# Loads of x and w1 dealt over two DMA rings, and a new order of block 0, in a dense layer with Mish

## The chip, the cores and the metric

The kernel runs on one core of a Trainium2 chip. The metric is the time that the device takes for one execution, in microseconds (us). The profile's span runs from the first to the last instruction of the core and is a little shorter than that time.

## The reference

x is 2048 x 512, w1 is 512 x 1792, b1 has 1792 elements, w2 is 1792 x 512; everything is bf16.

```python
h = jnp.einsum("bsd,df->bsf", x, w1) + b1
sp = jnp.log1p(jnp.exp(-jnp.abs(h))) + jnp.where(h > 0, h, jnp.zeros_like(h))
act = h * jnp.tanh(sp)                      # Mish
return jnp.einsum("bsf,fd->bsd", act, w2)
```

## The kernel before, in words

The 2048 rows of x are worked in four blocks of 512 rows (s = 0 to 3, each of four x tiles of 128 rows). For each block, mm1 makes h transposed: for each of the 14 f tiles (128 columns of w1) four matmuls over k (512 = 4 x 128) add up into one bank of PSUM, with w1 as the weights and x transposed (xT) as the moving operand. ScalarE's Mish with b1 as bias (`mish`, L152) writes a_sb, in the layout that mm2 needs as weights. mm2 (L191) then adds up 14 matmuls for each tile of 128 output rows, VectorE copies the result out of PSUM (L197), and SP writes it out (L200).

The order is written out by hand. Each engine has a `Stream`: `mark` counts up the engine's semaphore, `wait` puts a wait in front of the engine's next instruction. `free[bank]` holds what must have read a bank before TensorE may start a new sum in it. The profile names the tiles w1_sb and w2_sb both w_sb, b1_nat b_nat, b1_pad b_pad, b1_sb b_sb.

Loads. All use the helper at L84. ScalarE issues two parts of w1, f tiles 0-3 (F0 = 4) with k 0-1 and with k 2-3 (256 KB each), and then loads its table (L122). SP issues x tiles 0-1 in one load (x_nat, 256 KB; each partition takes two neighbouring rows, so the block's rows come interleaved and `rows` at L180 undoes that in the output), then a DMA transpose of x tiles 2-3 straight into xT (x23), f tiles 4-7 in two parts, b1, the rest of w1, w2, and the DMA transposes of blocks 1 to 3.

Block 0. TensorE runs seven dummy matmuls on a constant (WARM, L128) while it waits for x_nat. `transpose_x` (L135) then transposes x tiles 0-1 with eight TensorE transposes (L142); VectorE and ScalarE copy two banks each into xT (L145). `first` makes f tiles 0-3 in banks 4-7, first for x tiles 0-1 over all k, then for tiles 2-3. VectorE meanwhile copies b1 into b1_pad (L230). `half` makes f tiles 4-6 with k 0-1 in banks 0-2. Then TensorE transposes b1 into bank 3 (L234), and VectorE copies it to b1_sb (L236), which every Mish needs. Then `half` with k 2-3, and from f tile 7 on whole f tiles by `mm1`.

Of the kernel before, what the change touches and what calls it, by code (L numbers as in the profile page):

```python
# [4 lines left out]

P = 128
WARM = (512,) * 5 + (256, 256)
BLOCKS = (512, 512, 512, 512)


# [21 lines left out]
def bass_standalone__dense_activation_mish__prompt_kernel(  # L32
# [8 lines left out]
    ACT = mybir.ActivationFunctionType  # L41
    ALU = mybir.AluOpType
    BF, F32 = dt.bfloat16, dt.float32
# [3 lines left out]
    KT, FT = D // P, F // P  # L47
    assert (S, D, F) == (2048, 512, 1792) and sum(BLOCKS) == S
    x2, out2 = x[0], out[0]
# [3 lines left out]
    F0 = 4  # L53
    N0 = BLOCKS[0] // P

    with ExitStack() as es:
        def sb(name, shape, t):
            return es.enter_context(nc.sbuf_tensor(name, shape, t))

        x_nat = sb("x_nat", [P, 2, D], BF)  # L60
        xT = sb("xT", [P, KT, S], BF)
        w1_sb = sb("w1_sb", [P, KT, F], BF)
        w2_sb = sb("w2_sb", [P, FT, D], BF)
        b1_nat = sb("b1_nat", [FT, P], BF)
# [3 lines left out]
        ident = sb("ident", [P, P], BF)  # L68
        a_sb = sb("a_sb", [P, FT, S], BF)
        o_sb = sb("o_sb", [P, S // P, D], BF)  # L70
        ps = es.enter_context(nc.psum_tensor("ps", [P, 8, 512], F32))

        def sem(name):
            return es.enter_context(nc.semaphore(name))

        sp = Stream(nc.sync, None)
        pe = Stream(nc.tensor, sem("c_pe"))
        dve = Stream(nc.vector, sem("c_dve"))
        act = Stream(nc.scalar, sem("c_act"))
        pool = Stream(nc.gpsimd, sem("c_pool"))  # L80

        def load(q, dst, src, name, transpose=False):
            s = sem(name)
            (q.eng.dma_start_transpose if transpose else q.eng.dma_start)(dst, src).then_inc(s, 16)  # L84
            return (s, 16)

        def load_w1(q, ks, a, b):
            return load(q, w1_sb[:, ks, a * P:b * P], w1v[:, ks, a * P:b * P], "s_w1_%d_%d" % (ks.start, a))

        t_w1, t_w2 = {}, {}

        def load_part(q, k0, k1, a, b):
            t = load_w1(q, slice(k0, k1), a, b)
            for f in range(a, b):
                for k in range(k0, k1):
                    t_w1[k, f] = t

        for k0, k1 in ((0, 2), (2, 4)):  # L100
            load_part(act, k0, k1, 0, F0)
        t_xn = load(sp, x_nat[:, :, :], x2[0:2 * P, :].rearrange("(p j) d -> p j d", p=P), "s_xn")
        t_x23 = load(sp, xT[:, :, 2 * P:4 * P], x2[2 * P:4 * P, :], "s_x23", True)
        for k0, k1 in ((0, 2), (2, 4)):
            load_part(sp, k0, k1, F0, 8)
        t_b1 = load(sp, b1_nat[:, :], b1.rearrange("(j p) -> j p", p=P), "s_b1")
        load_part(sp, 0, KT, 8, FT)
        t = load(sp, w2_sb[:, :, :], w2v, "s_w2")
        for f in range(FT):
# [2 lines left out]
        for s in range(1, len(BLOCKS)):  # L112
            lo, hi = starts[s], starts[s + 1]
# [6 lines left out]
        t_id = pool.mark(pool.eng.affine_select(ident[:, :], ones[:, :], pattern=[[1, P]], compare_op=ALU.is_equal,  # L120
                                                fill=0.0, base=0, channel_multiplier=-1))
# [5 lines left out]
        def dummy(n):  # L127
            nc.tensor.matmul(ps[:, 7, 0:n], c_w, c_m[:, 0:n], start=True, stop=True)  # L128


        free = [[] for _ in range(8)]
        t_cp = {(j, k): t_x23 for j in (2, 3) for k in range(KT)}
        t_mish, t_acc = {}, {}

        def transpose_x():  # L135

            pe.wait(t_xn, t_id)
            for k in range(KT):
                eng = (dve, act)[k % 2]
                psb = ps[:, k, 0:P].bitcast(BF)  # L140
                for j in range(2):
                    mm = nc.tensor.transpose(psb[:, j * P:(j + 1) * P], x_nat[:, j, k * P:(k + 1) * P], ident[:, :])  # L142
                eng.wait(pe.mark(mm))
                dst = xT[:, k, 0:2 * P]
                t = eng.mark(nc.vector.tensor_copy(dst, psb) if eng is dve else act.eng.activation(dst, psb, ACT.Copy))  # L145
                t_cp[0, k] = t_cp[1, k] = t
                free[k] = [t]

        def mish(s, f, bank, t_mm):
            n = BLOCKS[s]  # L150
            act.wait(t_b1c, t_mm)
            t = act.mark(act.eng.activation(a_sb[:, f, starts[s]:starts[s + 1]], ps[:, bank, 0:n], ACT.Mish,  # L152
                                            bias=b1_sb[:, f:f + 1]))
            t_mish[s, f] = t
            free[bank] = [t]

        def mm1_step(s, f, k, bank, js=None):

            n = BLOCKS[s]
            lo, hi = (0, n) if js is None else (js[0] * P, (js[-1] + 1) * P)  # L160
            first = k == 0 and lo == 0
            if first:
                pe.wait(*free[bank])
            pe.wait(t_w1[k, f])
            if s:
                pe.wait(t_xT[s])
            else:
                pe.wait(*[t_cp[j, k] for j in (js or range(N0))])
            return nc.tensor.matmul(ps[:, bank, lo:hi], w1_sb[:, k, f * P:(f + 1) * P],  # L169
                                    xT[:, k, starts[s] + lo:starts[s] + hi], start=first, stop=(k == KT - 1 and hi == n))  # L170

        def mm1(s, f, bank):
            for k in range(KT):
                mm = mm1_step(s, f, k, bank)
            mish(s, f, bank, pe.mark(mm))

        s_out = sem("s_out")
        n_out = 0

        def rows(i):  # L180

            if i < 2:
                return out2[0:2 * P, :].rearrange("(p j) d -> p j d", p=P)[:, i, :]
            return out2[i * P:(i + 1) * P, :]

        def mm2_step(i, f, lo, hi, bank):
            s = max(b for b in range(len(BLOCKS)) if starts[b] <= i * P)
            if f == 0:
                pe.wait(*free[bank])
            pe.wait(t_w2[f], t_mish[s, f])  # L190
            return nc.tensor.matmul(ps[:, bank, 0:hi - lo], a_sb[:, f, i * P:(i + 1) * P], w2_sb[:, f, lo:hi],  # L191
                                    start=(f == 0), stop=(f == FT - 1))

        def put(i, lo, hi, bank, t_mm):
            nonlocal n_out
            dve.wait(t_mm)
            t = dve.mark(nc.vector.tensor_copy(o_sb[:, i, lo:hi], ps[:, bank, 0:hi - lo]))  # L197
            free[bank] = [t]
            sp.wait(t)
            sp.eng.dma_start(rows(i)[:, lo:hi], o_sb[:, i, lo:hi]).then_inc(s_out, 16)  # L200
            n_out += 1

        def mm2(i, lo, hi, bank):
            for f in range(FT):
                mm = mm2_step(i, f, lo, hi, bank)
            put(i, lo, hi, bank, pe.mark(mm))


        def first(js, ks):
            for k in ks:  # L210
                for f in range(F0):
                    mm = mm1_step(0, f, k, 4 + f, js)
                    if k == KT - 1 and js[-1] == N0 - 1:
                        t_acc[f] = pe.mark(mm)

        def half(fs, ks):
            for f in fs:
                for k in ks:
                    mm = mm1_step(0, f, k, f - F0)
                if ks[-1] == KT - 1:  # L220
                    t_acc[f] = pe.mark(mm)

        for n in WARM:
            dummy(n)
        transpose_x()
        first((0, 1), range(KT))
        first((2, 3), range(KT))

        dve.wait(t_b1, t_bz)
        t_b1p = dve.mark(nc.vector.tensor_copy(b1_pad[0:FT, :], b1_nat[:, :]))  # L230
        half(range(F0, F0 + 3), (0, 1))
        pe.wait(t_b1p, *free[3])
        psb1 = ps[:, 3, 0:P // 2].bitcast(BF)
        t_b1t = pe.mark(nc.tensor.transpose(psb1, b1_pad[:, :], ident[:, :]))  # L234
        dve.wait(t_b1t)
        t_b1c = dve.mark(nc.vector.tensor_copy(b1_sb[:, :], psb1[:, 0:FT]))  # L236
        free[3] = [t_b1c]
        for f in range(F0):
            mish(0, f, 4 + f, t_acc[f])
        half(range(F0, F0 + 3), (2, 3))  # L240
        for f in range(F0, F0 + 3):
            mish(0, f, f - F0, t_acc[f])
        for f in range(F0 + 3, FT):
            mm1(0, f, (4 + f) % 8)

        for i in range(N0):
# [39 lines left out]
```

## Time and profile before

| what | value |
|---|---|
| median of 3 runs | 105.65 us (104.71 to 105.7) |
| the profiled execution | 105.38 us |
| its span | 104.1 us |
| TensorE matmuls busy | 100.8 us, 97% |
| ScalarE busy | 39.1 us, 38% |
| VectorE busy | 12.3 us, 12% |
| moved by DMA | 7.94 MB |

How to read it: PE is TensorE, PEld its weight loads, ACT ScalarE, DVE VectorE; SPq and ACTq are the instructions by which SP and ScalarE issue DMAs. A row of the timeline gives start, duration, engine, line, operation, the tile written and the tiles read, the shape, how often, and in brackets how long the engine was idle before it and what ended that. The chain of work is followed back from the last instruction, each step to what released it. A row of the windows gives the length of the stretch, the busy time of each engine with its number of instructions, the granted clock, the DMA share and GB/s. A row of a DMA queue gives packets, MB and share of the 16 engines' time in the window.

### The profile page before, as it was taken

The page shows a single profiled execution, that of the slowest core. Times are in us where ns is not written, and L with a number is a line of the kernel's source. Part 1 is how long each engine was busy: PE and PEld are TensorE (multiplying, and loading weights), DVE is VectorE, ACT ScalarE, POOL GpSimd, SP SyncE. Part 2 cuts the span into 40 slices and gives each one's busy share as a digit, 9 for nine tenths or more (in the row PEclk, how much of TensorE's full clock was granted, in tenths as well). Part 3 has the DMA queues.
Part 4 walks back from the last instruction along what each step waited for, and adds up shares of the span by engine and source line. Part 5 has one row for each costly group of instructions (what it writes and reads, how often), then busy time and mean ns, then how long its engine had stood idle before and what let it go on. Part 6 is the DMA issues. An engine that isn't in the chain of part 4 may idle for free.

```text
span 104.1 us, 1118 instructions
## 1 busy us (share of the span) xinstructions
PE 100.8 (97%) x485; PEld 48.2 (46%) x494; DVE 12.3 (12%) x22; ACT 39.1 (38%) x59; POOL 0.7 (1%) x6
## 2 busy tenths in 40 slices
PE   6999999999999999999999999999999999999992
PEld 2586444444444444444444444444444444444462
DVE  0200000022220000022220000022112000011223
ACT  3400999200027777200007777500005777700000
POOL 2000000000000000000000000000000000000000
PEclk9999999999999999999999999999999999999999
DMA  2999999991101000010111000001111000001111
GB/s 42 331 337 362 347 320 131 211 193 50 43 7 50 0 0 0 6 50 2 49 50 50 0 0 3 0 6 50 50 50 50 0 0 0 0 0 50 57 50 50
DMA packets 13345, 7.94 MB, mean 76 GB/s; under 512 B 7836, under 2 KB 13212, under 8 KB 13340
## 3 DMA queue, kind: packets, MB, share of 16 engines
q1 hardware_dynamic: 12796, 7.35, 27.0%
q10 hardware_dynamic: 544, 0.52, 1.4%
q8 instruction: 4, 0.07, 0.3%
q14 instruction: 1, 0.01, 0.0%
HBM read 3.94 MB, written 2.10 MB: 58 GB/s over the span
## 4 chain that ended last, share of the span: by engine, by line
PE 94%; DMA 3%; issue 1%; DVE 0%
PE ps L169 47%; PE ps L191 46%; DMA x_nat<-in_x_dram 3%; PE ps L142 1%; DVE o_sb L197 0%; PE ps L234 0%
## 5 line engine op out<-in xcount | busy, mean ns | idle before, releaser
L152 ACT ACTIVATE a_sb<-ps,b_sb 128x512 bf16<-128x512 f32 x56 | 37.1, 697 | 48.6 <-PE ps L169 43.3
L169 PE MATMUL ps<-xT,w_sb 128*128 128x512 bf16 (+1 forms) x235 | 49.3, 368 | 0.2
L191 PE MATMUL ps<-w_sb,a_sb 128*128 128x512 bf16 (+2 forms) x234 | 48.8, 366 | 0.3
L169 PEld LDWEIGHTS ps<-xT,w_sb 128*128 128x128 bf16 x240 | 23.7, 99 | 24.9
L191 PEld LDWEIGHTS ps<-w_sb,a_sb 128*128 128x128 bf16 x238 | 22.8, 98 | 25.9
L197 DVE CAST o_sb<-ps 128x512 bf16<-128x512 f32 (+2 forms) x17 | 11.2, 660 | 80.9 <-PE ps L191 80.9
L128 PE MATMUL ps<-const-bfloat16-1.0 128*128 128x512 bf16 (+1 forms) x7 | 2.7, 564 | 0.8 <-PEq L271 0.8
L122 ACT ACT_TABLE_LOAD x1 | 1.3, 1283 | 1.8 <-issue 1.8
L128 PEld LDWEIGHTS ps<-const-bfloat16-1.0 128*128 128x128 bf16 x7 | 0.9, 134 | 2.2 <-issue 2.2
L145 ACT ACTIVATE xT<-ps 128x256 bf16<-128x256 bf16 x2 | 0.8, 384 | 1.4 <-PE ps L142 1.3
L142 PE MATMUL ps<-ident,x_nat 128*128 128x128 bf16 x8 | 1.0, 311 | 0.2 <-DMA x_nat<-in_x_dram 0.2
L142 PEld LDWEIGHTS ps<-ident,x_nat 128*128 128x128 bf16 x8 | 0.8, 140 | 0.7 <-DMA x_nat<-in_x_dram 0.7
L145 DVE COPY xT<-ps 128x256 bf16<-128x256 bf16 x2 | 0.6, 292 | 3.3 <-PE ps L142 3.2
L230 DVE COPY b_pad<-b_nat 14x128 bf16<-14x128 bf16 x1 | 0.2, 183 | 3.1 <-DMA b_nat<-in_b_dram 3.1
L236 DVE CAST b_sb<-ps 128x14 f32<-128x14 bf16 x1 | 0.2, 173 | 2.2 <-PE ps L234 2.2
L120 POOL TENSOR_SCALAR_AFFINE_SELECT ident<-ones 128x128 bf16<-128x128 bf16 x1 | 0.3, 295 | 0.1
L234 PE MATMUL ps<-ident,b_pad 128*128 128x128 bf16 x1 | 0.2, 219 | 0.0
L117 DVE MEMSET b_pad<- 128x64 uint32 x1 | 0.1, 112 | 0.9 <-PEq L271 0.9
L118 POOL MEMSET ones<- 128x128 bf16 x1 | 0.2, 205 | 0.3 <-POOLq L271 0.3
L234 PEld LDWEIGHTS ps<-ident,b_pad 128*128 128x128 bf16 x1 | 0.1, 98 | 0.1
L271 POOL MEMSET const-bfloat16-1.0<- 128x1 bf16 x1 | 0.1, 102 | 0.0
L271 POOL MEMSET const-uint8-127<- 128x1 uint8 x1 | 0.1, 102 | 0.0
(2 smaller groups left out, 0.2 us busy)
## 6 DMA issues: line engine op xcount, KB each, us to landing
out_dram<-o_sb SPq DMA_DIRECT2D x15, 128.0 KB, 1.7
w_sb<-in_w_dram SPq DMA_DIRECT2D x1, 1792.0 KB, 10.4
w_sb<-in_w_dram SPq DMA_DIRECT2D x1, 768.0 KB, 5.6
w_sb<-in_w_dram ACTq DMA_DIRECT2D x2, 256.0 KB, 3.8
w_sb<-in_w_dram SPq DMA_DIRECT2D x2, 256.0 KB, 4.4
x_nat<-in_x_dram SPq DMA_DIRECT2D x1, 256.0 KB, 2.9
out_dram<-o_sb SPq DMA_DIRECT2D x1, 96.0 KB, 1.6
xT<-in_x_dram SPq DMA_TRANSPOSE x4, 5.5
```

The source lines that it names most:

```text
L118: t_ones = pool.mark(pool.eng.memset(ones[:, :], 1.0))
L120: t_id = pool.mark(pool.eng.affine_select(ident[:, :], ones[:, :], pattern=[[1, P]], compare_op=ALU.is_equal, fill=0.0, base=0, channel_mu ...
L122: act.eng.preload_act_table(ACT.Mish)
L128: nc.tensor.matmul(ps[:, 7, 0:n], c_w, c_m[:, 0:n], start=True, stop=True)
L142: mm = nc.tensor.transpose(psb[:, j * P:(j + 1) * P], x_nat[:, j, k * P:(k + 1) * P], ident[:, :])
L145: t = eng.mark(nc.vector.tensor_copy(dst, psb) if eng is dve else act.eng.activation(dst, psb, ACT.Copy))
L152: t = act.mark(act.eng.activation(a_sb[:, f, starts[s]:starts[s + 1]], ps[:, bank, 0:n], ACT.Mish, bias=b1_sb[:, f:f + 1]))
L169: return nc.tensor.matmul(ps[:, bank, lo:hi], w1_sb[:, k, f * P:(f + 1) * P], xT[:, k, starts[s] + lo:starts[s] + hi], start=first, stop=( ...
L191: return nc.tensor.matmul(ps[:, bank, 0:hi - lo], a_sb[:, f, i * P:(i + 1) * P], w2_sb[:, f, lo:hi], start=(f == 0), stop=(f == FT - 1))
L197: t = dve.mark(nc.vector.tensor_copy(o_sb[:, i, lo:hi], ps[:, bank, 0:hi - lo]))
L230: t_b1p = dve.mark(nc.vector.tensor_copy(b1_pad[0:FT, :], b1_nat[:, :]))
L234: t_b1t = pe.mark(nc.tensor.transpose(psb1, b1_pad[:, :], ident[:, :]))
```

## The change

- x tiles 0 and 1 are loaded one by one (128 KB each, rows no longer interleaved): tile 0 on SP's ring, tile 1 on ScalarE's. Behind each comes one half of w1's f tiles 0-3: k 0-1 on SP, k 2-3 on ScalarE.
- b1 is the third load on ScalarE's queue, ahead of its table load, and no longer one of SP's.
- On SP, f tiles 4-7 with k 0-1 go ahead of the DMA transpose of x tiles 2-3; those with k 2-3 stay behind it.
- The warm-up is one 256-column matmul shorter.
- The transposes go by x tile: four for tile 0, four for tile 1, each bank taking two k's of one tile, and each copy writes two k's.
- mm1 of block 0 goes in another order: f tiles 0-3 with k 0-1 for x tile 0 alone, then for x tile 1 alone (128 columns each), then k 2-3 for both (256 columns); f tiles 4-5 with k 0-1 for x tiles 0-1; the transpose of b1; f tiles 6-7 likewise; then x tiles 2-3 for f tiles 0-3 (with their Mish), for f tiles 4-7 with k 0-1, and last k 2-3 of f tiles 4-7 over all 512 columns.
- The output rows are written in order for all tiles.

```diff
-WARM = (512,) * 5 + (256, 256)
+WARM = (512,) * 5 + (256,)
...
-        for k0, k1 in ((0, 2), (2, 4)):
-            load_part(act, k0, k1, 0, F0)
-        t_xn = load(sp, x_nat[:, :, :], x2[0:2 * P, :].rearrange("(p j) d -> p j d", p=P), "s_xn")
+        for q, j in ((sp, 0), (act, 1)):
+            t_xn[j] = load(q, x_nat[:, j, :], x2[j * P:(j + 1) * P, :], "s_xn%d" % j)
+            load_part(q, 2 * j, 2 * j + 2, 0, F0)
+        t_b1 = load(act, b1_nat[:, :], b1.rearrange("(j p) -> j p", p=P), "s_b1")
+        load_part(sp, 0, 2, F0, 8)
         t_x23 = load(sp, xT[:, :, 2 * P:4 * P], x2[2 * P:4 * P, :], "s_x23", True)
-        for k0, k1 in ((0, 2), (2, 4)):
-            load_part(sp, k0, k1, F0, 8)
-        t_b1 = load(sp, b1_nat[:, :], b1.rearrange("(j p) -> j p", p=P), "s_b1")
+        load_part(sp, 2, 4, F0, 8)
...
-        def transpose_x():
-            pe.wait(t_xn, t_id)
-            for k in range(KT):
-                eng = (dve, act)[k % 2]
-                psb = ps[:, k, 0:P].bitcast(BF)
-                for j in range(2):
-                    mm = nc.tensor.transpose(psb[:, j * P:(j + 1) * P], x_nat[:, j, k * P:(k + 1) * P], ident[:, :])
+        def transpose_x(j):
+            pe.wait(t_xn[j], t_id)
+            for h, eng in enumerate((dve, act)):
+                psb = ps[:, 2 * j + h, 0:P].bitcast(BF)
+                for i in range(2):
+                    k = 2 * h + i
+                    mm = nc.tensor.transpose(psb[:, i * P:(i + 1) * P], x_nat[:, j, k * P:(k + 1) * P], ident[:, :])
                 eng.wait(pe.mark(mm))
-                dst = xT[:, k, 0:2 * P]
+                dst = xT[:, 2 * h:2 * h + 2, j * P:(j + 1) * P]
...
-        transpose_x()
-        first((0, 1), range(KT))
-        first((2, 3), range(KT))
-
+        transpose_x(0)
+        transpose_x(1)
+        first(lo4, (0,), (0, 1))
+        first(lo4, (1,), (0, 1))
+        first(lo4, (0, 1), (2, 3))
         dve.wait(t_b1, t_bz)
         t_b1p = dve.mark(nc.vector.tensor_copy(b1_pad[0:FT, :], b1_nat[:, :]))
-        half(range(F0, F0 + 3), (0, 1))
+        first(hi4[:2], (0, 1), (0, 1))
+
         pe.wait(t_b1p, *free[3])
         psb1 = ps[:, 3, 0:P // 2].bitcast(BF)
         t_b1t = pe.mark(nc.tensor.transpose(psb1, b1_pad[:, :], ident[:, :]))
         dve.wait(t_b1t)
         t_b1c = dve.mark(nc.vector.tensor_copy(b1_sb[:, :], psb1[:, 0:FT]))
         free[3] = [t_b1c]
-        for f in range(F0):
-            mish(0, f, 4 + f, t_acc[f])
-        half(range(F0, F0 + 3), (2, 3))
-        for f in range(F0, F0 + 3):
-            mish(0, f, f - F0, t_acc[f])
-        for f in range(F0 + 3, FT):
+        for f in hi4[2:]:
+            first((f,), (0, 1), (0, 1))
+        first(lo4, (2, 3), range(KT - 1))
+        for f in lo4:
+            first((f,), (2, 3), (KT - 1,))
+            mish(0, f, 4 + f, pe.mark(t_acc[f]))
+        first(hi4, (2, 3), (0, 1))
+        for f in hi4:
+            first((f,), range(N0), (2, 3))
+            mish(0, f, f - F0, pe.mark(t_acc[f]))
+        for f in range(2 * F0, FT):
             mm1(0, f, (4 + f) % 8)
```

In the new `first(fs, js, ks)` f tile f goes to bank (4 + f) % 8: f tiles 4-7 to banks 0-3.

More of the change, by code (lines that the diff above doesn't have):

```diff
@@ L88, in load_w1 @@
             return load(q, w1_sb[:, ks, a * P:b * P], w1v[:, ks, a * P:b * P], "s_w1_%d_%d" % (ks.start, a))
-        t_w1, t_w2 = {}, {}
+        t_xn, t_w1, t_w2 = {}, {}, {}
         def load_part(q, k0, k1, a, b):
@@ L133, in bass_standalone__dense_activation_mish__prompt_kernel @@
         t_mish, t_acc = {}, {}
-        def transpose_x():
-            pe.wait(t_xn, t_id)
-            for k in range(KT):
-                eng = (dve, act)[k % 2]
-                psb = ps[:, k, 0:P].bitcast(BF)
-                for j in range(2):
-                    mm = nc.tensor.transpose(psb[:, j * P:(j + 1) * P], x_nat[:, j, k * P:(k + 1) * P], ident[:, :])
-                eng.wait(pe.mark(mm))
-                dst = xT[:, k, 0:2 * P]
-                t = eng.mark(nc.vector.tensor_copy(dst, psb) if eng is dve else act.eng.activation(dst, psb, ACT.Copy))
-                t_cp[0, k] = t_cp[1, k] = t
-                free[k] = [t]
+        def transpose_x(j):
[5 more added lines that the diff above has]
+                    mm = nc.tensor.transpose(psb[:, i * P:(i + 1) * P], x_nat[:, j, k * P:(k + 1) * P], ident[:, :])
+                eng.wait(pe.mark(mm))
+                dst = xT[:, 2 * h:2 * h + 2, j * P:(j + 1) * P]
+                src = psb.rearrange("p (k t) -> p k t", k=2)
+                t = eng.mark(nc.vector.tensor_copy(dst, src) if eng is dve else act.eng.activation(dst, src, ACT.Copy))
+                for i in range(2):
+                    t_cp[j, 2 * h + i] = t
+                free[2 * j + h] = [t]
         def mish(s, f, bank, t_mm):
@@ L178, in bass_standalone__dense_activation_mish__prompt_kernel @@
         n_out = 0
[L180 to L184, printed above, removed]
         def mm2_step(i, f, lo, hi, bank):
@@ L199, in put @@
             sp.wait(t)
-            sp.eng.dma_start(rows(i)[:, lo:hi], o_sb[:, i, lo:hi]).then_inc(s_out, 16)
+            sp.eng.dma_start(out2[i * P:(i + 1) * P, lo:hi], o_sb[:, i, lo:hi]).then_inc(s_out, 16)
             n_out += 1
@@ L206, in mm2, with first @@
             put(i, lo, hi, bank, pe.mark(mm))
-        def first(js, ks):
+        def first(fs, js, ks):
             for k in ks:
-                for f in range(F0):
[L212 to L221, printed above, removed]
+                for f in fs:
+                    t_acc[f] = mm1_step(0, f, k, (4 + f) % 8, js)
+        lo4, hi4 = range(F0), range(F0, 2 * F0)
         for n in WARM:
             dummy(n)
-        transpose_x()
-        first((0, 1), range(KT))
-        first((2, 3), range(KT))
+        transpose_x(0)
[3 more added lines that the diff above has]
+        first(lo4, (0, 1), (2, 3))
         dve.wait(t_b1, t_bz)
         t_b1p = dve.mark(nc.vector.tensor_copy(b1_pad[0:FT, :], b1_nat[:, :]))
-        half(range(F0, F0 + 3), (0, 1))
+        first(hi4[:2], (0, 1), (0, 1))
         pe.wait(t_b1p, *free[3])
@@ L237, in bass_standalone__dense_activation_mish__prompt_kernel @@
         free[3] = [t_b1c]
-        for f in range(F0):
-            mish(0, f, 4 + f, t_acc[f])
-        half(range(F0, F0 + 3), (2, 3))
-        for f in range(F0, F0 + 3):
-            mish(0, f, f - F0, t_acc[f])
-        for f in range(F0 + 3, FT):
+        for f in hi4[2:]:
[9 more added lines that the diff above has]
+        for f in range(2 * F0, FT):
             mm1(0, f, (4 + f) % 8)
```

## The prediction

> **What bounds the kernel now.** I read the page first (busy shares and the chain that ended last), then the chain in order of time, then the timeline of the first 12 us, then the DMA view cut to short windows. The page and the chain of work say this:
>
> ```profile
> PE 100.8 (97%) x485; PEld 48.2 (46%) x494; DVE 12.3 (12%) x22; ACT 39.1 (38%) x59; POOL 0.7 (1%) x6
> ...
> PE 94%; DMA 3%; issue 1%; DVE 0%
> ```
>
> ```profile
> 0.80 2.92 DMA x_nat<-in_x_dram
> ...
> 3.77 1.03 PE ps L142 x8
> 4.80 4.58 PE ps L169 x34
> ...
> 10.24 0.06 PE ps L234
> 10.30 7.34 PE ps L169 x34
> ...
> 95.61 6.69 PE ps L191 x44
> 102.29 0.02 issue
> 102.32 0.29 DVE o_sb L197
> ```
>
> The reader should see one engine without a gap. From 3.77 us, when x_nat has landed, to 102.3 us TensorE is the chain, and nothing else is on it but short issue pieces. So the change, which touches only the first 12 us, can move the end in two ways only: TensorE starts its real work earlier or later, or it gets or loses an idle stretch. The timeline of that stretch:
>
> ```profile
> 0.79 0.99 ACTq L84 DMA_DIRECT2D w_sb<-in_w_dram  x2
> ...
> 0.80 0.40 SPq L84 DMA_DIRECT2D x_nat<-in_x_dram  x1
> ...
> 0.83 2.72 PE L128 MATMUL ps<-const-bfloat16-1.0 128*128 128x512 bf16 x7 [0.83 <-PEq L271]
> ...
> 1.26 1.30 SPq L84 DMA_TRANSPOSE xT<-in_x_dram  x1
> ...
> 1.82 1.28 ACT L122 ACT_TABLE_LOAD   x1 [1.82 <-issue]
> ...
> 2.62 1.08 SPq L84 DMA_DIRECT2D w_sb<-in_w_dram  x2
> ...
> 3.77 1.03 PE L142 MATMUL ps<-ident,x_nat 128*128 128x128 bf16 x8 [0.21 <-DMA x_nat<-in_x_dram]
> 4.20 0.72 DVE L145 COPY xT<-ps 128x256 bf16<-128x256 bf16 x2 [3.21 <-PE ps L142]
> ...
> 4.41 0.81 ACT L145 ACTIVATE xT<-ps 128x256 bf16<-128x256 bf16 x2 [1.31 <-PE ps L142]
> ...
> 4.64 5.61 PE L169 MATMUL ps<-xT,w_sb 128*128 128x256 bf16 x37
> ```
>
> The first product of mm1 starts at 4.64. It needs three things: the transposes, VectorE's first copy (4.20 plus half of 0.72, so about 4.5), and the first part of w1. Next, the same 256-column matmuls in two windows (columns: length, TensorE busy and count):
>
> ```profile
> 4.64:5.87 1.23, 1.23 (x6) 0.86 (x7) 1.00 1.31 287
> 6.05:8.78 2.73, 2.73 (x27) 2.45 (x25) 1.00 1.09 363
> ```
>
> Six in 1.23 us is 0.21 us each; 27 in 2.73 us is 0.10 us each. Up to about 6.0 us TensorE runs at half speed, although the clock column shows 1.00 in both. So an instant gained or lost before 6.0 us is worth half of itself, and one after it the whole.
>
> **The DMA side.** Issue to landing: the first two rows are ScalarE's loads of w1 (issued 0.79 and 1.29), the third is the transpose of x tiles 2-3 (issued 1.26), the fourth x_nat (issued 0.80).
>
> ```profile
> w_sb<-in_w_dram ACTq DMA_DIRECT2D x1, 256.0 KB, 3.7
> ```
>
> ```profile
> w_sb<-in_w_dram ACTq DMA_DIRECT2D x1, 256.0 KB, 4.0
> xT<-in_x_dram SPq DMA_TRANSPOSE x1, 5.0
> ```
>
> ```profile
> x_nat<-in_x_dram SPq DMA_DIRECT2D x1, 256.0 KB, 2.9
> ```
>
> So x_nat landed at 3.7, the halves of w1 at 4.5 and 5.3, and x tiles 2-3 at 6.3. The first half of w1 landed as late as VectorE's first copy: the start of mm1 at 4.64 stands on two legs, and shortening one gains nothing. How the two rings share the engines is seen in the queue rows of four windows (1.80:2.85, 2.90:3.25, 3.3:4.2, 4.28:4.60; q1 is SP's ring, q10 ScalarE's):
>
> ```profile
> q1 hardware_dynamic: 100, 0.20, 90.5%
> ```
>
> ```profile
> q10 hardware_dynamic: 76, 0.08, 63.4%
> q1 hardware_dynamic: 36, 0.05, 38.4%
> ```
>
> ```profile
> q10 hardware_dynamic: 344, 0.34, 106.1%
> q1 hardware_dynamic: 1, 0.00, 0.1%
> ```
>
> ```profile
> q1 hardware_dynamic: 179, 0.05, 62.9%
> q10 hardware_dynamic: 66, 0.05, 49.9%
> ```
>
> Both rings were issued into at 0.79 and 0.80, yet until 2.85 only SP's x_nat moved; then 3.3 to 4.2 was ScalarE's alone, although SP's transpose had been issued by 2.56. The rings took turns by whole transfers, and packets of both mixed only at a change-over.
>
> **The change part by part.** The sum is made against the profiled execution: 105.38 us, with a span of 104.1. The median of the three runs, 105.65, is 0.27 above it.
>
> *x in two tiles, one on each ring; half of w1's f tiles 0-3 behind each.* The bytes ahead of the first half of w1 are the same 256 KB as before. If transfers go on taking turns whole (x tile 0, x tile 1, first half of w1 on SP, second half on ScalarE), x tile 0 lands some 0.3 earlier than x_nat did (half the bytes), at about 3.4, x tile 1 at 3.7, and the first half of w1 at 4.5 as before. The transposes start about 0.4 earlier and then wait: mm1 starts at 4.5 + 0.1 = 4.6 against 4.64. I take 0. The best end: w1 lands early and mm1 follows the transposes, which start when the dummies end at about 3.35 (0.83 + 2.72 = 3.55 less the removed 0.2) and take 0.87 to mm1 (3.77 to 4.64): 4.22, so 0.42 at half weight, -0.21. The worst end: the two halves move packet by packet as in the last window above, so that the first lands with the second, at 5.3: mm1 at 5.4, 0.76 at half weight, +0.38. I take the value near 0 because three of the four windows show turns by whole transfers.
>
> *Warm-up shorter by one 256-column matmul.* Nothing by itself: TensorE waited for x_nat until 3.77 anyway. Its cover is the landing of x tile 0.
>
> *Transposes and copies by tile.* Still eight transposes, and two copies each of 128x256 on VectorE and ScalarE; only the destination has two rows of 128. Nothing, since the sizes are those of the rows at 4.20 and 4.41.
>
> *b1 third on ScalarE's queue.* A third issue there (0.99/2 = 0.5) moves the table load from 1.82 to about 2.3, its end to 3.6. ScalarE's first copy can't start before about 3.35 + 0.43 + 0.17 = 3.95, so 0.35 of cover; and what it makes (k 2-3) is first read by the 17th matmul, 1.7 us after the first. Nothing.
>
> *f tiles 4-7, k 0-1, ahead of the transpose.* SP now issues x tile 0, two parts of w1, then the transpose at about 2.3 instead of 1.26, and the same number of issues in all (b1 leaves, a part of w1 comes), so w1's rest, w2 and the later x blocks go out and land as before. Landing of x tiles 2-3: 2.3 + 5.0 = 7.3 instead of 6.3. In the new order they are wanted after 16 matmuls of 128 columns, 16 of 256 and the transpose of b1: from 4.6, with the speed doubling at 6.0, 1.7 + 0.9 + 0.4 + 0.1 + 0.4 comes to about 8.2. A margin of 0.9; beyond it each us costs a whole one.
>
> *More, smaller matmuls.* Block 0 has 88 instead of 72. At the tail, 128-column matmuls stand so:
>
> ```profile
> 101.33:102.10 0.77, 0.77 (x16) 0.77 (x13) 0.56 (x1) 0.00 (x0) 0.00 (x0) 1.00 0.00 0
> ```
>
> That is 0.05 each, half of a 256-column one, so splitting is nearly free: +0.03.
>
> *The transpose of b1 in bank 3.* This is the edit that I think costs. Before, f tiles 4-6 used banks 0-2, and f 7 came to bank 3 much later. Now f 6 (bank 2) and f 7 (bank 3) come right behind the transpose of b1 into bank 3, so f 7's first matmul waits for VectorE's copy out of it. The rows of before:
>
> ```profile
> 10.08 0.22 PE L234 MATMUL ps<-ident,b_pad 128*128 128x128 bf16 x1
> ...
> 10.34 0.17 DVE L236 CAST b_sb<-ps 128x14 f32<-128x14 bf16 x1 [2.17 <-PE ps L234]
> 10.54 0.69 ACT L152 ACTIVATE a_sb<-ps,b_sb 128x512 bf16<-128x512 f32 x1 [5.32 <-DVE b_sb L236]
> ```
>
> From the transpose's start to the first reader of the copy's result: 10.54 - 10.08 = 0.46, plus a weight load's start (about 0.03). TensorE has in between 0.06 + 2 x 0.109 = 0.28 of work. Idle: 0.2, at full speed. Bounds: 0 (if it would have waited for x tiles 2-3 there anyway) to 0.3. Queued behind the waiting matmul is all of TensorE's work.
>
> *Mish earlier, output rows in order.* The first Mish comes some 0.6 earlier than 10.54; ScalarE is busy 38% and not on the chain. The output writes keep their number and row length. Nothing; the cover is that TensorE ends last.
>
> Sum: 0 + 0.03 + 0.2 = +0.23, so 105.6 against 105.38; carried half-way to the median of the runs, **105.8**.
>
> **Two rules of the Trainium skill.** Its page "DMA: Bandwidth & Descriptors", section "Issuing engines are not separate DMA queues", says that DMAs issued from several engines run on the same 16 engines and interleave, so that spreading them saves only issue time. By it the two halves of w1 land together, mm1 starts at 5.4 and the sum would be 106.0; the first and third window above speak against it, the last for it. Its page "TensorE: Matmul & The Clock Gate", section on the clock gate, says that the full clock is granted after a free-running window of about 3.4 us in which TensorE was busy. By it a window missed would put the doubling 3.4 later and cost 1.7 (an estimate from that figure), 107.3; no run here shows a missed window.
>
> **The rivals.**
> 1. *The halves of w1 interleave, the doubling of speed stays at 6.0.* For it: the mixed window at 4.28:4.60. Against it: 0.8 to 2.85 and 3.3 to 4.2. mm1 at 5.4: 105.6 + 0.38 = 106.0; still within 1% of the median.
> 2. *The doubling of speed comes later (the slower side).* Before, it came 5.2 us after the first dummy (0.83 to 6.0) across a hole of 0.2 to 0.4 before the transposes. Now the dummies end 0.2 sooner and a second hole opens between transposes and mm1: 0.4 in my likeliest case, about 1.1 with interleaved halves. If the holes make the count begin anew at the transposes, at about 3.8, the doubling comes at 3.8 + 5.2 = 9.0, 3.0 later, and costs 1.5: 107.1. It decides (over 1%) from a delay of about 2 us. Against it: a hole of like size was borne before. It goes well with rival 1.
> 3. *x tiles 2-3 late.* The transpose would have to take 6 us instead of 5.0; at 7 us it costs 1.0: 106.6.
> 4. *An earlier start after all.* -0.21 with the stall at b1 left: 105.4. Only if the doubling also came at the start of mm1 would (6.0 - 4.64)/2 = 0.68 more be gained: 104.7.
>
> **How the numbers follow.** Runs of this kernel differ by 1.0 us (104.71 to 105.7), and I read 1% (1.06 us) as about what a measurement can tell from no change. Chances: my forecast 0.50; rival 1 0.17; rival 2 0.18; rival 3 0.04; rival 4 0.11. Slower by over 1% (above 106.7) gets rival 2 and some of 1 and 3: 0.25. Faster by over 1% (below 104.6) is only the far end of rival 4 and scatter: 0.07. The rest, 0.68, is within 1%. The range: 104.9 leaves out the far end of rival 4, 107.1 half of rival 2. The likeliest case alone would lie in 105.2 to 106.2.
>
> **What would show it.** x tile 0's transposes before 3.6; mm1's first matmul at 4.5 to 4.7 (5.3 or later is rival 1); an idle stretch of 0.2 on TensorE behind the transpose of b1, released by VectorE; none at x tiles 2-3; 256-column matmuls at 0.109 from about 6 us on (from 9: rival 2). A gap-free TensorE behind b1 would refute the one cost I name, and a first mm1 at 4.2 would refute the two legs.

## The result, and the profile after

| | before | after |
|---|---|---|
| median of 20 executions each | 105.32 us (104.71 to 105.85) | 106.21 us (105.09 to 107.92) |
| ratio, 95% interval | | 1.0056 [1.0029, 1.0082] |
| the profiled execution, its span | 105.38, 104.1 us | 107.31, 106.1 us |

So the change made the kernel about half a per cent slower by the ratio, which is less than the 1% that the prediction took as what a measurement can tell from no change. The ratio sets aside executions over 1.5% above a kernel's fastest, six of the 20 after (the profiled one, 107.31, is among them) and none before, so that the medians over all of them stand further apart, by 0.8%.

The page of the changed kernel (engine busy times, chain by engine):

```profile
PE 102.7 (97%) x509; PEld 50.0 (47%) x509; DVE 12.3 (12%) x22; ACT 39.3 (37%) x59; POOL 0.7 (1%) x6
...
PE 93%; DMA 3%; DVE 0%; SPq 0%; issue 0%
```

Its chain of work, in order of time:

```profile
1.26 3.65 DMA w_sb<-in_w_dram
...
4.95 4.37 PE ps L171 x28
9.32 0.07 PE ps L224
...
9.41 0.18 DVE b_sb L226
...
9.64 9.92 PE ps L171 x58
```

TensorE is still the chain, but what it waits for at the start is no longer x: it is SP's half of w1, landed at 4.91. And there is a new link, VectorE's copy of b1 at 9.41. The timeline:

```profile
0.80 0.41 ACTq L84 DMA_DIRECT2D x_nat<-in_x_dram  x1
...
0.81 0.39 SPq L84 DMA_DIRECT2D x_nat<-in_x_dram  x1
...
0.84 2.50 PE L128 MATMUL ps<-const-bfloat16-1.0 128*128 128x512 bf16 x6 [0.84 <-PEq L266]
...
1.24 0.46 ACTq L84 DMA_DIRECT2D w_sb<-in_w_dram  x1
1.26 0.93 SPq L84 DMA_DIRECT2D w_sb<-in_w_dram  x2
...
3.42 1.04 PE L142 MATMUL ps<-ident,x_nat 128*128 128x128 bf16 x8
...
4.95 4.37 PE L171 MATMUL ps<-xT,w_sb 128*128 128x128 bf16 x28 [0.49 <-DMA w_sb<-in_w_dram]
...
9.64 3.38 PEld L171 LDWEIGHTS ps<-xT,w_sb 128*128 128x128 bf16 x30 [0.33 <-DVE b_sb L226]
```

Three things differ from before. The transposes start at 3.42 instead of 3.77, and nothing comes of it: they end at 4.46, and TensorE idles 0.49 until mm1 starts at 4.95 (before: 4.64, without a wait). Behind the transpose of b1 there is a wait for VectorE. And the doubling of TensorE's speed, seen in three windows of mm1 alone (length, TensorE busy and count; 128 columns in the first, 256 in the others; a count takes in the matmuls still running when its window opens):

```profile
4.95:6.60 1.65, 1.65 (x16) 1.65 (x17) 1.00 1.22 261
6.63:8.98 2.35, 2.35 (x13) 1.67 (x12) 1.00 1.06 315
9.22:11.50 2.28, 2.23 (x20) 1.77 (x20) 1.00 1.09 361
```

13 matmuls in 2.35 us up to 8.98, 20 in 2.28 behind it: here the doubling came at about 9.1, not at 6.0. Both profiled executions can be reconciled: doubling 3.1 later at half weight 1.55, mm1 0.31 later at half weight 0.16, the wait behind b1 0.21, together 1.92 of the 1.93 between 105.38 and 107.31. In the executions without the later doubling the last two terms alone make 0.37, or 0.52 where the clock doubles before mm1 starts and its 0.31 counts whole (an estimate from the same rows). By the ratio the kernel is 0.59 us behind, so part of that isn't accounted for.

Why w1 was late is in the queue rows of the window 3.25:4.50:

```profile
q10 hardware_dynamic: 244, 0.24, 55.3%
q1 hardware_dynamic: 222, 0.21, 49.0%
```

ScalarE's and SP's halves of w1 went out together, about one packet for one. The transpose of x tiles 2-3 was issued at 2.23 and took:

```profile
xT<-in_x_dram SPq DMA_TRANSPOSE x1, 4.9
```

It landed at 7.1 and nothing waited for it.

### The profile page after: what moved, and what is told of

Same layout as the page of the kernel before. It is cut to its first block, busy times and chain, and to the rows that moved or that the text cites. A ratio compares the mean times of both kernels' runs of the same rounds, so it can differ in the third digit from the quotient of the medians.

```text
span 106.1 us, 1158 instructions
## 1 busy us (share of the span) xinstructions
PE 102.7 (97%) x509; PEld 50.0 (47%) x509; DVE 12.3 (12%) x22; ACT 39.3 (37%) x59; POOL 0.7 (1%) x6
## 4 chain that ended last, share of the span: by engine, by line
PE 93%; DMA 3%; DVE 0%; SPq 0%; issue 0%
PE ps L171 48%; PE ps L187 46%; DMA w_sb<-in_w_dram 3%; SPq L84 0%; DVE o_sb L193 0%; DVE b_sb L226 0%; PE ps L224 0%
## 5 line engine op out<-in xcount | busy, mean ns | idle before, releaser
L171 PE MATMUL ps<-xT,w_sb 128*128 128x512 bf16 (+2 forms) x256 | 51.3, 365 | 0.5 <-DMA w_sb<-in_w_dram 0.5
L171 PEld LDWEIGHTS ps<-xT,w_sb 128*128 128x128 bf16 x256 | 25.5, 103 | 25.4 <-DMA w_sb<-in_w_dram 0.8
```

## The experiments

Each kernel was timed beside the kernel before on the same chip. "Late" counts executions above 106.8 us; of 119 executions of the kernel before in all these comparisons none is, though the highest stands just under it at 106.78, and so do two of e7. It counts times, not doublings: an execution can be late for another wait as well (e9). "Idle" is TensorE's idle time in the profiled execution between the first dummy and its first steady stretch of mm1, from the brackets of the timeline or the gap between rows.

| kernel | mm1 starts | idle | late | ratio to before |
|---|---|---|---|---|
| before | 4.64 | 0.21 | 0 of 119 | 1 |
| after | 4.95 | 0.57 | 6 of 20 | 1.0056 [1.0029, 1.0082] |
| after again (e11) | 4.90 | 0.53 | 4 of 6 | 1.0175 [1.0130, 1.0220] |
| filler (e1) | 4.98 | 0.16 | 1 of 12 | 1.0072 [1.0038, 1.0105] |
| b1 early (e2) | 5.02 | 0.65 | 3 of 12 | 1.0054 [1.0021, 1.0087] |
| w1 dealt by k (e3) | 4.51 | 0.29, later 0.23 | 0 of 12 | 1.0083 [1.0050, 1.0115] |
| e1 to e3 together (e4) | 4.57 | 0.18 | 0 of 12 | 1.0054 [1.0028, 1.0080] |
| filler and b1 early (e10) | 4.87 | 0.17 | 0 of 12 | 1.0023 [0.9992, 1.0054] |
| before, short warm-up (e5) | 4.57 | 1.42 | 1 of 6 | 1.0111 [1.0064, 1.0158] |
| before, long warm-up (e12) | 4.88 | 0.24 | 0 of 12 | 1.0013 [0.9983, 1.0042] |
| before, w1 dealt (e8) | 5.71 | 1.12 | 6 of 12 | 1.0055 [1.0023, 1.0087] |
| w1 on ScalarE's ring (e6) | 4.82 | 0.51 | 6 of 12 | 1.0034 [0.9994, 1.0074] |
| e6, x23 first, b1 early (e7) | 4.79 | 0.65 | 3 of 12 | 1.0098 [1.0055, 1.0140] |
| before, x split (e9) | 4.64 | 0.34, later 2.12 | 4 of 6 | 1.0155 [1.0116, 1.0195] |

### The hole before mm1: e1, e10, e11

e1 fills it with two dummies:

```diff
         transpose_x(1)
+        for n in (256, 256):
+            dummy(n)
         first(lo4, (0,), (0, 1))
```

> The changed kernel with two more dummy matmuls of 256 columns between the transposes and the first matmul of mm1, so that TensorE has no hole there while it waits for w1. Theory A (the hole of 0.5 us before mm1 makes TensorE's doubling of speed come a few us later in some executions): the doubling comes by 7 us, the spread shrinks to about that of the kernel before (1.1 us), no time above 106.8, median 105.7 to 105.9, ratio to before about 1.004. Rival B (the doubling does not depend on holes; only the late mm1 and the wait behind b1's transpose cost): median and spread as in the changed kernel, 106.2 with times up to 107.9.

Measured: 105.35 to 107.41, median 105.85, one execution of 12 late. Eleven do as theory A says; one doesn't, so "none above 106.8" fell. This alone didn't settle it. Nor does the ratio, which leaves the late executions out. e10 closes the hole with three dummies and also takes the wait behind b1 away (the edit of e2); e11 is the changed kernel itself, on the same chip.

> The changed kernel with filler matmuls (256, 256 and 128 columns) that close the hole before mm1, and the transpose of b1 ahead of f tiles 4-5; loads as changed. Theory (two separate costs): no late doublings and no idle stretch behind b1; mm1 still starts at 4.95, so at the same instant of doubling it stands 0 to 0.3 over the kernel before; ratio to before 1.002 to 1.005, no time above 106.8. Rival (the late doublings come from something else): a quarter of the executions above 107.

> The changed kernel itself, on the chip of the two others, as their yardstick: mm1 at 4.9 to 5.0, 0.21 idle behind b1, a quarter to a third of the executions above 107, ratio to before 1.003 to 1.008.

Measured: e10 105.0 to 106.19, none late, 1.0023; e11 106.19 to 107.73, 1.0175 [1.0130, 1.0220]. e11 came out slower than expected, and more often late, and its ratio has its four late executions in it; e10 came out as expected. With the loads unchanged, filling the hole and taking away the wait is worth 1.5% on this chip, and none of e10's executions is above any of e11's. e10 makes both edits at once. For the hole as what makes executions late speak the counts: with the filler and otherwise the loads of the change (e1, e10) one in 24 was late, without it (after, e11, e2) 13 in 38. e11's start of mm1, and e10's stretch without an idle bracket from its transposes on:

```profile
4.90 4.45 PE L171 MATMUL ps<-xT,w_sb 128*128 128x128 bf16 x28 [0.35 <-DMA w_sb<-in_w_dram]
```

```profile
3.52 1.03 PE L142 MATMUL ps<-ident,x_nat 128*128 128x128 bf16 x8 [0.17 <-DMA x_nat<-in_x_dram]
...
4.34 0.74 PE L128 MATMUL ps<-const-bfloat16-1.0 128*128 128x256 bf16 x3
4.87 2.87 PE L171 MATMUL ps<-xT,w_sb 128*128 128x128 bf16 x24
...
7.58 0.22 PE L224 MATMUL ps<-ident,b_pad 128*128 128x128 bf16 x1
7.63 2.57 PE L171 MATMUL ps<-xT,w_sb 128*128 128x256 bf16 x22
```

### The hole alone, in the kernel before: e5, e12

```diff
-WARM = (512,) * 5 + (256, 256)
+WARM = (512,) * 3
```

> The kernel before with three dummy matmuls instead of seven, so that TensorE has a hole of about 1.3 us ahead of the transposes and is otherwise unchanged. Theory A (a hole early on lets the doubling of TensorE's speed come later): mm1 starts at 4.64 as before, but the doubling comes after 7 us in a part or most of the executions, with times of 106.5 to 108; ratio to before above 1.005. Rival B (the doubling does not depend on holes): same times as before, 1.000.

Measured: 105.62 to 106.92, 1.0111 [1.0064, 1.0158]. mm1 starts as before (4.57), no load was touched, and yet the doubling came only between 8.5 and 8.85 in the profiled execution (two windows of mm1):

```profile
4.75:8.50 3.75, 3.75 (x19) 2.69 (x18) 1.00 1.14 319
8.85:11.00 2.15, 2.15 (x18) 1.55 (x16) 1.00 1.09 357
```

Fewer dummies, and with them a hole of 1.42 us ahead of the transposes, are enough to delay the doubling; theory B is out. The times were a little lower than expected, and only one is above 106.8. e12 goes the other way and adds a dummy (`(512,) * 5 + (256, 256, 256)`):

> The kernel before with eight dummy matmuls instead of seven (one more of 256 columns), which closes its own hole of about 0.4 us ahead of the transposes. Theory (a hole matters only from some length on, between 0.4 and 0.7 us, where a late doubling sets in): same as before, ratio 0.998 to 1.002, mm1 at 4.6. Rival (every hole delays the doubling by its length): 0.1 to 0.2 us faster, ratio 0.998 or less.

Measured: 1.0013 [0.9983, 1.0042], no difference. In its profiled execution x_nat landed at 4.0, so 0.24 of idle was left even so, and mm1 started at 4.88. That is no less than the 0.21 of the kernel before, so the edit didn't close the hole there, and whether it did in the other executions isn't known. What the small hole costs therefore stays open.

### The wait behind the transpose of b1: e2

```diff
-        first(hi4[:2], (0, 1), (0, 1))
         pe.wait(t_b1p, *free[3])
...
-        for f in hi4[2:]:
+        for f in hi4:
             first((f,), (0, 1), (0, 1))
```

> The changed kernel with the transpose of b1 moved ahead of f tiles 4-5, so that six matmuls instead of two stand between it and the first user of its bank. Theory (the wait for VectorE's copy out of bank 3 costs 0.2): the idle stretch of 0.21 behind the transpose is gone and nothing takes its place, since x tiles 2-3 have landed by then; 0.2 less than the changed kernel at the same instant of doubling, ratio to before about 1.003. Rival (TensorE would have waited there for x tiles 2-3 or b1 anyway): the idle stretch moves, same time as the changed kernel, 1.0056.

Measured: the wait is gone (the row of mm1 behind b1's transpose has no bracket), and nothing took its place:

```profile
8.40 0.31 PE L222 MATMUL ps<-ident,b_pad 128*128 128x128 bf16 x1
8.51 2.75 PE L171 MATMUL ps<-xT,w_sb 128*128 128x256 bf16 x21
```

The ratio, 1.0054, is that of the rival (1.0056) rather than the 1.003 of the theory, but its interval can't tell 0.2 us from nothing; the hole is left in this kernel and so are its late executions. The size rests on the trace: 0.323 between two matmuls that otherwise stand 0.109 apart, in the changed kernel.

### Who shares the engines with whom: e3, e8, e6, e7

e3 deals w1 so that both rings first carry what mm1 needs first:

```diff
-            load_part(q, 2 * j, 2 * j + 2, 0, F0)
+            load_part(q, j, j + 1, 0, F0)
+        for q, j in ((sp, 2), (act, 3)):
+            load_part(q, j, j + 1, 0, F0)
```

> The changed kernel with w1's f tiles 0-3 dealt by k: k 0 and k 2 on SP, k 1 and k 3 on ScalarE (128 KB each), so that both rings carry what mm1 needs first. Theory (the rings take turns packet by packet, so the half needed first landed nearly with the other): k 0-1 land at about 4.4 instead of 4.9, mm1 starts at about 4.5, the hole is about 0.2, 0.2 to 0.3 less than the changed kernel at the same instant of doubling, late doublings rarer; ratio to before about 1.002. Rival (the late landing is the latency of a second load on a ring, not the sharing): 4.9 again, no gain.

Measured: as the theory has it for the first half, mm1 starts at 4.51 and no execution is late. But the gain didn't come (1.0083): k 2, now the third load on SP's ring beside f tiles 4-7, landed at 6.1, and TensorE waited for it.

```profile
4.51 1.44 PE L173 MATMUL ps<-xT,w_sb 128*128 128x128 bf16 x16
...
6.18 1.48 PE L173 MATMUL ps<-xT,w_sb 128*128 128x256 bf16 x12 [0.23 <-DMA w_sb<-in_w_dram]
```

e4 puts the edits of e1 (with two dummies of 128 columns), e2 and e3 together.

> The three edits together (dummies of 128 columns as filler). If the three costs are separate and add up: mm1 at 4.5, no wait behind b1's transpose, doubling by 7 us: 105.1 to 105.3, ratio to before 0.997 to 1.000. If one cost only hides another: 1.002 or more.

Measured: mm1 at 4.57, no wait behind b1, doubling at 6.7 in the profiled execution, and 1.0054: by its ratio the second of its two cases. None of its 12 executions is under 105.2 us (the kernel before: 104.45 on that chip). The late k 2 of e3 could set such a floor. In the profiled execution of e4 it landed late too, at about 6.0, but mm1 came to it only at 6.28 and didn't wait; no kernel here takes it away, so this isn't shown.

e8 makes one edit to the kernel before: the first half of w1 goes behind x_nat on SP's ring, the second half first on ScalarE's.

> The kernel before with one edit: the first half of w1's f tiles 0-3 moved behind x_nat on SP's ring, the second half first on ScalarE's. Theory (dealt over two rings, they take turns packet by packet with x_nat and with each other): the first half lands at about 4.9 or later instead of 4.5, x_nat later than 3.7 as well, mm1 starts at 5.0 or later, ratio 1.003 to 1.008, with some late doublings. Rival (whole loads take turns as in the kernel before): the first half lands by 4.6, no change.

Measured: x_nat at 4.2 instead of 3.7, mm1 at 5.71, six of 12 late:

```profile
4.27 1.03 PE L142 MATMUL ps<-ident,x_nat 128*128 128x128 bf16 x8 [0.71 <-DMA x_nat<-in_x_dram]
...
5.71 6.27 PE L169 MATMUL ps<-xT,w_sb 128*128 128x256 bf16 x34 [0.41 <-DMA w_sb<-in_w_dram]
```

The doubling came at about 10.2 there (two windows of mm1):

```profile
5.90:10.20 4.30, 4.30 (x22) 3.05 (x21) 1.00 1.08 347
10.40:12.60 2.20, 2.15 (x16) 1.37 (x14) 1.00 1.09 346
```

So dealing w1 over the rings is harm enough by itself, as the theory said (here x_nat shares the engines as well). e6 undoes only the dealing: both x tiles on SP, both halves of w1 on ScalarE.

```diff
-        for q, j in ((sp, 0), (act, 1)):
-            t_xn[j] = load(q, x_nat[:, j, :], x2[j * P:(j + 1) * P, :], "s_xn%d" % j)
-            load_part(q, 2 * j, 2 * j + 2, 0, F0)
+        for j in range(2):
+            t_xn[j] = load(sp, x_nat[:, j, :], x2[j * P:(j + 1) * P, :], "s_xn%d" % j)
+            load_part(act, 2 * j, 2 * j + 2, 0, F0)
```

> The changed kernel with both x tiles on SP's ring and both halves of w1's f tiles 0-3 on ScalarE's, in order, then b1: the dealing over the rings undone, all else as changed. Theory (two rings share the engines packet by packet, one ring works off its loads in order): the first half lands at about 4.5 and mm1 starts at 4.6 instead of 4.95, without a hole; no execution has a late doubling; ratio to before 1.000 to 1.003 (the wait behind b1's transpose, 0.2, is left). Rival (f tiles 4-7 on SP, now third there and ahead of the transpose, share the engines with the first half too): it lands at about 4.8 to 4.9 and mm1 starts at 4.9, ratio 1.005.

Measured: both theories missed. w1's first half is in time (4.0), but now x tile 1, second on SP, shares with it and lands at 4.4; the hole moves between the two tiles' transposes, and half the executions are late:

```profile
4.42 0.61 PE L142 MATMUL ps<-ident,x_nat 128*128 128x128 bf16 x4 [0.51 <-DMA x_nat<-in_x_dram]
...
4.82 2.55 PE L171 MATMUL ps<-xT,w_sb 128*128 128x128 bf16 x28
```

e7 adds the edit of e2 and puts the DMA transpose ahead of f tiles 4-7 again.

> As the run with both halves on ScalarE's ring, and in addition the DMA transpose of x tiles 2-3 ahead of f tiles 4-7 again and the transpose of b1 ahead of f tiles 4-5. Theory (late first half, and wait behind b1, are all that the change cost): mm1 at 4.5 to 4.6, no idle stretch behind b1, x tiles 2-3 landed by 6.6 and not waited for; ratio to before 0.998 to 1.001. If something else in the change costs as well: 1.003 or more.

Measured: 1.0098. The same hole (x tile 1 at 4.5), and f tiles 4-5 waited 0.47 for their w1, which landed at 7.2. Moving the transpose ahead has a price in the new order of block 0.

### x split in the kernel before: e9

The kernel before with x tile 0 on SP and tile 1 on ScalarE, both halves of w1 behind tile 1, the DMA transpose second on SP, transposes and first matmuls by tile, warm-up one shorter.

> The kernel before with x split as in the change (tile 0 on SP's ring, tile 1 on ScalarE's, transposes by tile, the first matmuls by tile, warm-up one shorter), but with both halves of w1's f tiles 0-3 behind each other on ScalarE's ring, the transpose of x tiles 2-3 second on SP, b1 on SP and the old order of the rest. Theory (sharing by packets made w1's first half late; the split of x is good by itself): x tiles land at 3.4 and 3.6, the first half of w1 at 4.2 to 4.4, mm1 starts at 4.4 to 4.5 without a hole above 0.2, no late doublings, ratio to before 0.998 to 1.000. If the split of x is the harm: a hole and late doublings, ratio above 1.003.

Measured: 106.31 to 109.03, 1.0155. x at 3.6 and 3.8, w1's first half only at 4.6, mm1 at 4.64, and the second half at 8.1: the DMA transpose ran beside it, and the engines moved 78 GB/s in 4.64:5.26, against 232 in the same window of the kernel before. TensorE waited 2.12 us, so the theory's forecast failed. In this trace alone the clock column shows what the others only let one infer (four windows; behind the busy times granted clock, DMA share, GB/s):

```profile
4.64:5.26 0.62, 0.62 (x8) 0.62 (x8) 0.19 (x1) 0.45 (x2) 0.00 (x0) 1.00 1.42 78
...
8.85:12.00 3.15, 3.15 (x16) 2.21 (x15) 0.18 (x1) 0.00 (x0) 0.00 (x0) 0.50 1.07 362
```

```profile
8.66:8.71 0.05, 0.05 (x3) 0.04 (x2) 0.00 (x0) 0.00 (x0) 0.00 (x0) 1.00 1.31 440
8.73:8.78 0.05, 0.05 (x3) 0.05 (x1) 0.00 (x0) 0.00 (x0) 0.00 (x0) 0.50 1.32 420
12.07:12.12 0.05, 0.05 (x2) 0.05 (x1) 0.00 (x0) 0.00 (x0) 0.00 (x0) 0.50 1.10 348
12.15:12.20 0.05, 0.05 (x2) 0.04 (x1) 0.00 (x0) 0.00 (x0) 0.00 (x0) 1.00 1.10 348
```

The clock fell to a half at 8.72, after TensorE had idled, and rose again at about 12.13, 3.4 us later. The first doubling lies as far ahead: matmuls of 128 columns start 0.107 us apart up to 5.26 and 0.056 from 5.34 on, which is 3.4 before 8.72. So half speed is the granted clock, and in this trace it changes in steps of 3.4 us. By the ratio the second case (the split of x is the harm) came true, but the longest wait, 2.12, is for w1. Whether the split of x is good by itself stays open: this kernel brought the transpose into the way.

## Why the prediction was right, and where it was wrong

The time (106.21 for 105.8, within 104.9 to 107.1) and the sign were right; the mechanism that I called likeliest was not. That the number came so near is in part luck. It stands on a median of three, 105.65, which 20 executions put at 105.32, and the rise that I forecast, 0.15 to 0.23, is well under the 0.59 that the ratio gives; the median of 106.21 is lifted further by the late executions, which are rival 2's. By its steps:

- *What bounds the kernel, and half weight before the doubling.* Right: the profiled pair adds up with these weights, 1.92 of 1.93. An execution whose clock doubles before mm1 starts pays the whole (e1: 28 matmuls from 4.98 in 2.38 us, all at full speed).
- *x in two tiles; w1's halves dealt; "I take the value near 0 because three of the four windows show turns by whole transfers".* This step failed. x tiles landed as foreseen (3.4 and 3.6), but the halves of w1 shared packet by packet and mm1 started at 4.95, 0.31 late, where I took 0 and gave 5.4 as the end; it lies between my sign for the forecast (4.5 to 4.7) and that for rival 1 (5.3). Two of my windows showed only one ring at work, which is no evidence of how two share: in the kernel before ScalarE's ring had nothing moving before 2.85. The second and fourth windows, where both had packets, were the ones to go by. So was the rule of the Trainium skill's page "DMA: Bandwidth & Descriptors" (section "Issuing engines are not separate DMA queues") that DMAs of different engines interleave. The runs agree with it: 244 and 222 packets in 1.25 us.
- *The doubling comes later (rival 2, 0.18).* It happened in a part of the executions, and its price was about right: 1.5 forecast and 1.55 in the profiled pair, 107.1 forecast and 107.16 to 107.92 measured in the six late ones. My condition for it was met by the step that failed. My count, begun anew at the transposes, doesn't hold: it puts the doubling 5.2 us behind their start, and in e8 it came 5.9 behind (4.27 to about 10.2). The rule of the Trainium skill's page "TensorE: Matmul & The Clock Gate" (Part 1, "The HAM clock gate": free-running windows of about 3.4 us) fits better. e9 shows the 3.4 us, and e5 that a late doubling needs no late load.
- *b1 in bank 3, 0.2.* Right in place and size: 0.323 instead of 0.109 between two matmuls, 0.21; gone in e2 and e10.
- *x tiles 2-3 with a margin of 0.9.* Right: landed at 7.1, not waited for. With the doubling at 6.0 the last three of the first 16 matmuls already run at full speed, so the sum comes to about 8.0 rather than 8.2 and the margin to 0.7; it decided nothing.
- *Edits at nothing (shorter warm-up, b1 on ScalarE's queue, copies, Mish, output).* In no trace does TensorE wait for any of them. The first Mish, foreseen 0.6 earlier than 10.54, came at 11.56 in the profiled execution, behind the late doubling, and nothing waited for it. With the shorter warm-up I counted on x tile 0 to cover it, and it did: 0.08 of idle. But idle time before the doubling can have a second price that the chain of work doesn't show: it adds to the hole.

What stays open: how much idle time in a window is too much. Kernels with 0.16 to 0.29 us of it in the profiled execution were late once in 60 executions (and the kernel before in none of 119), those with 0.5 and more 29 times in 80 (e9 left out, where a wait of 2.12 us makes executions late by itself). I drew these groups after the runs, and executions other than the profiled ones have no trace. The hole's length alone doesn't decide: e6's profiled execution had 0.51 of it and doubled in time, its first 28 matmuls taking 2.55 us against 4.37 in the changed kernel. If the clock steps every 3.4 us everywhere, as in e9, one can count back from each doubling (an estimate, one execution each): e6 bore 0.51 in the stretch from 1.6 to 5.0, while 0.57 in 2.3 to 5.7 was too much for the changed kernel and 0.53 in 2.6 to 6.0 for e11. Where the steps fall in an execution would then make it late or not.

## What to carry to other kernels

Two rings serve their heads at the same time, so of two loads dealt over them the first comes nearly as late as the second (4.9 and 5.1 us here). Loads that are needed one after the other are therefore better kept behind each other on one ring, or each dealt over both; but look at what then shares with what. Both were tried here (e6, e3), each made another load late, and no order tried was faster than the kernel before. While the tensor engine's clock is still at a half, fill a hole of half a microsecond with dummy work: the hole costs half its length by the chain, and about 1.5 us more where the doubling comes 3.1 us later, as in the changed kernel. A copy out of a bank that the next sum needs wants as much other work between as its latency, here 0.46 us.

## What the runs showed of the hardware that I had not expected

- In e9 a DMA transpose beside a plain load of another ring ran with both slowed: 78 GB/s in 4.64:5.26, 7.1 us for the transpose instead of 5.0, and the second half of w1 at 8.1 instead of 5.3. In the kernel before the two also shared the engines, in 4.28:4.60, at 313 GB/s. So the company alone isn't the cause, which stays open.
- The clock column of a profile can read 1.00 while matmuls run at half rate: 13 in 2.35 us in the changed kernel, at 1.00. Only e9, where the clock fell again, shows 0.50.
- The doubling has an instant of its own in each execution: with 0.24, 0.21, 0.18 and 0.17 us of idle ahead of it, it came at 5.6 (e12), 6.0 (before), 6.7 (e4) and 6.8 (e10), while e8's profiled execution still ran at half speed at 10.2 (22 matmuls of 256 columns in 5.90:10.20). The kernel before spreads over 1.1 us; differing instants would fit that, but only one of its executions has a trace.
